# One of four sums of activations: from an adding transfer to an add on VectorE, and a longer landing in the planner's table

## The chip, the core and the metric

The kernel runs on one core of a Trainium2 chip. The metric is the device time of one execution in microseconds; the time before is 1039.71 us, the median of three runs (1039.67 to 1039.81). TensorE's granted clock was 0.999 of its full rate in the profiled execution.

## The reference

Three stages follow one another, all in float32.

1. Attention over channels: q, k and v are 6016 x 256. The columns of q and k are divided by their norm over the 6016 rows, s = k^T q / tau is 256 x 256, a softmax is taken over its last axis, and v is multiplied by the result.
2. First layer: h = x w_in (256 to 2048 channels), g = h * clip(h + 3, 0, 6) / 6, and g w_out back to 256 channels.
3. Second layer: h = max(x w_in2, 0), and (h * h) w_out2.

```
    h = np.maximum(x @ w_in, 0.0)
    return (h * h @ w_out).astype(np.float32)
```

## The kernel before, in words

**The work.** The tokens are cut into six pairs of blocks, five of 2 x 512 and one of 2 x 448 tokens. A pair goes through the 2048 hidden channels in eight groups of 256. One pair and one group is a unit; the second layer has 48 of them. Every float32 operand is split into a high and a low half (float32r), and a product is three matmuls: high x high, low x high, high x low. A split is made of a copy on ScalarE (the high half) and a subtraction on VectorE (the low half).

Both matrix products of a unit, 2 x 2 blocks each, can be formed by seven products in place of eight from sums of blocks (Strassen's scheme, Winograd's form). From the second pair of the second layer on, first7s (L1558) forms the hidden layer of a unit by seven products p1 to p7 in two PSUM banks, X and Y. ScalarE takes snapshots of a bank into SBUF (snap, L1589), VectorE adds totals from a bank (total, L1595), then the rectifier and the square follow (L1602, L1608 on ScalarE, L1615 on VectorE for one block). The four blocks of the hidden layer stand in four tiles R[0] to R[3]; the tiles of even units are called rs in the trace, those of odd units rp.

**Seven products in the second half of a unit.** In 19 of the 40 such units (even groups; S2SET, L1434) the output product is made by seven products too. It needs four sums of the hidden blocks, here called data sums. tail (L1677) forms them in place, one after the other: t1 = R[1] + R[0] in R[1], t3 = R[0] + R[2] in R[0], t2 = R[1] + R[2] in R[1], t4 = R[3] + R[1] in R[3]. Each sum is split for TensorE (split, L1619: high half L1623, low half L1627) into a tile called gs. A sum overwrites its tile only after the tile's own split has read it. The sums are made by move (L1635): a DMA issued from GpSimd's queue (L1637) that adds its source to its destination, 128 x 512 float32, 256 KB. Here the sums of a unit are four such transfers. t1 waits for the split of R[1] and the square of R[0]; t3 waits for t1; t2 waits for the split of t1; t4 waits for t2. In the list of the planner t2 depends on t3 as well, though it reads nothing that t3 writes.

The tail of unit k is entered in the program when unit k+2 is; its products are placed in unit k+3 (items_sums, L1751): t3's at the beginning, those of t2, t1 and t4, in that order, at the end. The weights' sums for them (w2x) are made ahead of the stretch.

**The order of the work.** Plan (L22) lays out the order of every engine by hand. Each operation has an engine, a cost and a latency (how long after its end its users may start). TensorE and the DMA issues of SyncE keep the order in which the program lists them. For VectorE, ScalarE and GpSimd, issue (L66) runs through the program by these costs: the engine that can start first takes, of its ready operations, the one whose due time is earliest. Due times are reckoned back from the products on TensorE that need the result. The order found is then written out; on the chip each engine runs its list strictly in order and waits for whatever its next instruction needs. A move is entered with a cost of MOVE_US = 0.9 us on GpSimd and a latency of MOVE_LAT = 4.2 us (L155), an operation on VectorE over n columns with dve_us(n) = 0.07 + 0.00104 n, one on ScalarE with act_us(n) = 0.1 + 0.00083 n.

While this goes on SyncE issues the loads of weights (w from w1d, 448 KB each), of the next pair's tokens (xr from x2d, 256 KB each) and the stores of results, on the same 16 DMA engines.

Of the kernel before, what the change touches and what calls it, by code (L numbers as in the profile page):

```python
# [15 lines left out]
ALU = mybir.AluOpType  # L16
# [11 lines left out]
class Plan:  # L28
# [13 lines left out]
    def add(self, eng, cost, fn, *deps, lat=LAT):  # L42

        o = Op(eng, cost, lat, fn, list(deps))
        self.ops.append(o)
        return o
# [91 lines left out]
def dve_us(n):  # L138
    return 0.07 + 0.00104 * n
# [12 lines left out]
    return 0.15 + 0.0012 * n  # L152


MOVE_US, MOVE_LAT = 0.9, 4.2  # L155


def pe_us(n, passes):
# [5 lines left out]
def tile_kernel(  # L164
# [71 lines left out]
    V, A, T_ = nc.vector, nc.scalar, nc.tensor  # L236
    plan = Plan()
    add = plan.add
# [699 lines left out]
    for i in range(NCH):  # L938
        loads = chunk_load(i)
        t0, n = chunks[i]  # L940
# [617 lines left out]
    def first7s(pr, g):  # L1558

        l, n = 1, pairs[pr][1]  # L1560
# [4 lines left out]
        R = sets[g // 2 % len(sets)]  # L1565
        names = ("d0", "d1", "d2", "d3") if even else ("p0", "p1", "p2", "p3")
        X, Y = cells["X"], cells["Y"]
        u = {"n": n, "pr": pr, "g": g, "seven": seven, "R": R}

        def product(into, start, wn, xn, *deps):  # L1570
            p = x_op[l, pr, xn]

            def f():
                wh, wl = w_p["w"][:, 0, OPW[wn]], w_p["w"][:, 1, OPW[wn]]
                xh, xl = p["x"][:, 0, :n], p["x"][:, 1, :n]
                ps = into.ap()[:, :n]
                T_.matmul(ps, wh, xh, start=start, stop=False, skip_group_check=True)  # L1577
                T_.matmul(ps, wl, xh, start=False, stop=False, skip_group_check=True)  # L1578
                T_.matmul(ps, wh, xl, start=False, stop=True, skip_group_check=True)  # L1579

            o = add("PE", pe_us(n, 3), f, w_ok, x_done[l, pr, xn], *deps)
            x_held[l, pr, xn].append(o)
            w1_held[l, pr, g].append(o)
            return o

        def snap(k, bank, mm, *deps):
            return add(
                "ACT", act_us(n),
                lambda: A.activation(R[k].ap()[:, :n], bank.ap()[:, :n], AF.Copy), mm, *deps,  # L1589
            )  # L1590

        def total(k, bank, *deps):
            def f():
                r = R[k].ap()[:, :n]
                V.tensor_tensor(r, bank.ap()[:, :n], r, ALU.add)  # L1595

            return add("DVE", dve_us(n), f, *deps)

        def relu(k, src, *deps):
            return add(  # L1600
                "ACT", act_us(n) + 0.08,
                lambda: A.activation(R[k].ap()[:, :n], src.ap()[:, :n], AF.Relu), *deps,  # L1602
            )

        def square(k, *deps):
            def f():
                r = R[k].ap()[:, :n]
                A.activation(r, r, AF.Square)  # L1608

            return add("ACT", act_us(n), f, *deps)  # L1610

        def both(k, *deps):
            def f():
                r = R[k].ap()[:, :n]
                V.scalar_tensor_tensor(r, r, 0.0, r, ALU.max, ALU.mult)  # L1615

            return add("DVE", dve_us(n), f, *deps)

        def split(k, cell, *deps):  # L1619
            c = cells[cell]  # L1620

            def f_hi():
                A.activation(c.ap()[:, 0, :n], R[k].ap()[:, :n], AF.Copy)  # L1623

            def f_lo():
                x = c.ap()
                V.tensor_tensor(x[:, 1, :n], R[k].ap()[:, :n], x[:, 0, :n].bitcast(F32), ALU.subtract)  # L1627

            hi = add("ACT", act_us(n), f_hi, *deps, c.take())
            lo = add("DVE", dve_us(n), f_lo, hi)  # L1630
            R[k].use(hi, lo)
            c.use(hi, lo)
            return c, hi, lo

        def move(k, j, *deps):  # L1635
            def f():
                nc.gpsimd.dma_start(R[k].ap()[:, :n], R[j].ap()[:, :n], accum_op=ALU.add)  # L1637

            o = add("POOL", MOVE_US, f, *deps, lat=MOVE_LAT)
            R[k].use(o)  # L1640
            R[j].use(o)
            return o

        def steps():
            p1 = product(X, True, "a11", "b11", X.take())
            sn1 = snap(0, X, p1, R[0].take())
            yield
            p2 = product(Y, True, "a12", "b21", Y.take())
            h11 = total(0, Y, p2, sn1)
            Y.use(h11)  # L1650
            g0 = square(0, relu(0, R[0], h11))
            if not seven:
                u[0] = split(0, names[0], g0)
            yield
            p6 = product(X, False, "s2", "t2", sn1)
            sn6 = snap(2, X, p6, R[2].take())
            yield
            p7 = product(Y, True, "s3", "t3", Y.take())
            sn7 = snap(3, Y, p7, R[3].take())
            yield  # L1660
            p5 = product(X, False, "s1", "t1", sn6)
            h22 = total(3, X, p5, sn7)
            g3 = both(3, h22)
            u[3] = split(3, names[3], g3)
            yield
            p4 = product(Y, False, "a22", "t4", sn7)
            h21 = total(2, Y, p4, sn6)
            Y.use(h21)
            g2 = square(2, relu(2, R[2], h21))
            u[2] = split(2, names[2], g2)  # L1670
            yield
            p3 = product(X, False, "s4", "b22", h22)
            r = relu(1, X, p3, R[1].take())
            X.use(r)
            g1 = square(1, r)
            u[1] = split(1, names[1], g1)
            def tail():  # L1677
                t1 = move(1, 0, u[1][1:], g0)
                u["t1"] = split(1, "t1", t1)
                t3 = move(0, 2, t1, g2)  # L1680
                u["t3"] = split(0, "t3", t3)
                t2 = move(1, 2, u["t1"][1:], t3)
                u["t2"] = split(1, "t2", t2)
                t4 = move(3, 1, t2, u[3][1:])
                u["t4"] = split(3, "t4", t4)

            if seven:
                u["tail"] = tail
            yield
# [362 lines left out]
```

## Time and profile before

| what | value |
|---|---|
| median of three runs | 1039.71 us (1039.67 to 1039.81) |
| the profiled execution | 1039.63 us, its span 1037.8 us |
| granted clock of TensorE | 0.999 |
| TensorE busy | 1023.2 us, 4565 matmuls |
| VectorE busy | 858.1 us, 1353 instructions |
| ScalarE busy | 795.0 us, 1287 instructions |
| GpSimd busy | 85.9 us, 97 instructions, of them 76 adding transfers |

The span is the time from the first to the last instruction of the core; the execution's own time is a little longer. An engine's busy time says how much it works, not whether it holds up the others. In the timeline, a bracket at the end of a row gives how long the engine was idle before the instruction and what ended that idle time. Rows of GpSimd's transfers show the time in which the engine issues them; their landing is told apart. Rows of matmuls overlap, since they are pipelined: what counts is the distance between their starts.

### The profile page before, as it was taken

How to read it: one execution, taken by the hardware profiler on the slowest of the kernel's cores; microseconds unless marked ns; L12 is line 12 of the kernel's file. 1: busy time of each engine (PE TensorE's matmuls, PEld its weight loads, DVE VectorE, ACT ScalarE, POOL GpSimd, SP SyncE). 2: the span in 40 equal slices, each digit the busy share in tenths (PEclk: the TensorE clock that was granted, in tenths of full speed). 3: DMA queues.
4: the chain of work that ended last, by engine and by line, in shares of the span. 5: the costliest groups of instructions: out<-in, count | busy, mean ns of one | idle time of the engine just before them, and what ended most of it. 6: DMA issues, size and time to landing. Idle time of an engine off the chain costs nothing.

```text
span 1037.8 us, 13028 instructions
## 1 busy us (share of the span) xinstructions
PE 1023.2 (99%) x4565; PEld 853.0 (82%) x4565; DVE 858.1 (83%) x1353; ACT 795.0 (77%) x1287; POOL 85.9 (8%) x97
## 2 busy tenths in 40 slices
PE   9999999999999999999999999999999999999998
PEld 7888888888888888888998888788777778878897
DVE  3999988889989898898878976788778878868866
ACT  5787667678677777677668878888788879778784
POOL 3400000000000000000000000111111111112110
PEclk9999999999999999999999999999999999999999
DMA  9657346344545545635645334765757675765761
GB/s 357 262 174 247 126 152 228 132 159 166 190 150 168 188 146 170 236 107 205 226 167 181 114 107 132 187 176 147 204 130 170 160 190 138 189 172 136 191 169 46
DMA packets 65345, 178.98 MB, mean 172 GB/s; under 512 B 7296, under 2 KB 10880, under 8 KB 64000
## 3 DMA queue, kind: packets, MB, share of 16 engines
q1 hardware_dynamic: 54336, 158.62, 45.4%
q0 software_dynamic: 10944, 19.53, 10.9%
q8 instruction: 36, 0.59, 0.2%
q14 instruction: 29, 0.24, 0.1%
HBM read 126.35 MB, written 32.24 MB: 153 GB/s over the span
## 4 chain that ended last, share of the span: by engine, by line
PE 69%; issue 14%; DMA 13%; POOL 2%; DVE 1%; ACT 0%; SPq 0%; POOLq 0%
DMA rs<-rs 12%; PE acc L1362 10%; PE acc L1367 10%; PE acc L1361 10%; PE A L1268 4%; PE A L1269 4%; PE A L1270 4%; PE s L900 3%; POOL rs L1637 2%; PE B L1270 2%; PE B L1269 2%; PE B L1268 2%; PE xy L1577 2%; PE xy L1578 2%; PE xy L1579 2%
## 5 line engine op out<-in xcount | busy, mean ns | idle before, releaser
L1361 PE MATMUL acc<-g,wo 128*128 128x512 f32 (+1 forms) x448 | 172.9, 386 | 0.0
L1362 PE MATMUL acc<-g,wo 128*128 128x512 f32 (+1 forms) x448 | 172.9, 386 | 0.0
L1154 DVE TENSOR_TENSOR g<-r,g 128x1024 fp32r<-128x1024 f32 (+1 forms) x112 | 135.0, 1205 | 24.0 <-ACT g L1150 23.8
L1150 ACT ACTIVATE g<-r 128x1024 fp32r<-128x1024 f32 (+1 forms) x112 | 117.1, 1046 | 46.1 <-DVE r L1124 45.4
L1637 POOL DMA_DIRECT2D rs<-rs x76 | 65.7, 864 | 907.6 <-DVE gs L1627 775.2
L1367 PE MATMUL acc<-g,wo 128*128 128x512 f32 (+1 forms) x448 | 136.5, 386 | 0.0
L1627 DVE TENSOR_TENSOR gs<-rs,gs 128x512 fp32r<-128x512 f32 (+1 forms) x137 | 90.3, 674 | 42.3 <-ACT gs L1623 40.8
L1623 ACT ACTIVATE gs<-rs 128x512 fp32r<-128x512 f32 (+1 forms) x137 | 80.4, 614 | 22.1 <-DMA rs<-rs 16.0
L1362 PEld LDWEIGHTS acc<-g,wo 128*128 128x128 f32 x448 | 84.1, 188 | 16.1
L1361 PEld LDWEIGHTS acc<-g,wo 128*128 128x128 f32 x448 | 84.1, 188 | 16.1
L1367 PEld LDWEIGHTS acc<-g,wo 128*128 128x128 f32 x448 | 84.1, 188 | 16.1
L1119 ACT ACTIVATE r<-hp,three 128x1024 f32<-128x1024 f32 (+1 forms) x40 | 45.3, 1132 | 49.0 <-DVE hp L1301 48.9
L1577 PE MATMUL xy<-xt,w 128*128 128x512 f32 (+1 forms) x160 | 64.0, 400 | 7.4 <-ACT rs L1589 4.5
L1293 ACT ACTIVATE hp<-A 128x512 f32<-128x512 f32 (+1 forms) x96 | 56.6, 589 | 9.6 <-PE A L1270 8.6
L1578 PE MATMUL xy<-xt,w 128*128 128x512 f32 (+1 forms) x160 | 61.7, 386 | 0.0
L1579 PE MATMUL xy<-xt,w 128*128 128x512 f32 (+1 forms) x160 | 61.6, 385 | 0.0
L1124 DVE SCALAR_TENSOR_TENSOR r<-r,hp 128x1024 f32<-128x1024 f32 (+1 forms) x40 | 47.9, 1197 | 15.8 <-ACT r L1119 15.5
L1627 DVE TENSOR_TENSOR gs<-rp,gs 128x512 fp32r<-128x512 f32 (+1 forms) x80 | 52.5, 671 | 5.8 <-ACT gs L1623 5.1
L1707 PE MATMUL acc<-gs,wo 128*128 128x512 f32 (+1 forms) x141 | 54.3, 385 | 0.0
L1708 PE MATMUL acc<-gs,wo 128*128 128x512 f32 (+1 forms) x141 | 54.3, 385 | 0.0
L1709 PE MATMUL acc<-gs,wo 128*128 128x512 f32 (+1 forms) x141 | 54.2, 385 | 0.0
L1623 ACT ACTIVATE gs<-rp 128x512 fp32r<-128x512 f32 (+1 forms) x80 | 49.1, 615 | 4.5 <-DVE rp L1615 4.0
(375 smaller groups left out, 2595.3 us busy)
## 6 DMA issues: line engine op xcount, KB each, us to landing
w<-w1d SPq DMA_DIRECT2D x176, 448.0 KB, 4.3
rs<-rs POOLq DMA_DIRECT2D x64, 256.0 KB, 3.5
qk<-in_qk_dram SPq DMA_DIRECT2D x8, 1024.0 KB, 16.3
w1d<-wA SPq DMA_DIRECT2D x16, 448.0 KB, 5.3
xr<-in_vT_dram SPq DMA_DIRECT2D x5, 1024.0 KB, 6.8
x2d<-o SPq DMA_DIRECT2D x20, 256.0 KB, 3.9
w1d<-wA SPq DMA_DIRECT2D x16, 256.0 KB, 2.6
w1d<-w SPq DMA_DIRECT2D x14, 256.0 KB, 2.7
```

What stands on the lines that cost most here:

```text
L1150: A.activation(t["g"][:, a:b, 0, :n], t["t"][:, a:b, :n], AF.Copy)
L1154: V.tensor_tensor(g[:, a:b, 1, :n], t["t"][:, a:b, :n], g[:, a:b, 0, :n].bitcast(F32), ALU.subtract)
L1268: T_.matmul(ps, wh, xh, start=start, stop=False, skip_group_check=True)
L1361: T_.matmul(acc[b, e][:, :n], w(e, 0), gh_, start=first_of, stop=False)
L1362: T_.matmul(acc[b, e][:, :n], w(e, 1), gh_, start=False, stop=False)
L1367: T_.matmul(acc[b, e][:, :n], w(e, 0), gl_, start=False, stop=last_of_b)
L1577: T_.matmul(ps, wh, xh, start=start, stop=False, skip_group_check=True)
L1578: T_.matmul(ps, wl, xh, start=False, stop=False, skip_group_check=True)
L1579: T_.matmul(ps, wh, xl, start=False, stop=True, skip_group_check=True)
L1623: A.activation(c.ap()[:, 0, :n], R[k].ap()[:, :n], AF.Copy)
L1627: V.tensor_tensor(x[:, 1, :n], R[k].ap()[:, :n], x[:, 0, :n].bitcast(F32), ALU.subtract)
L1637: nc.gpsimd.dma_start(R[k].ap()[:, :n], R[j].ap()[:, :n], accum_op=ALU.add)
```

## The change

The first of the four data sums, t1, is no longer a transfer but a tensor_tensor of VectorE, in place, with the same two tiles and the same dependencies: it is entered with dve_us(n) as its cost and the ordinary latency. t3, t2 and t4 stay transfers. The readers and writers of both tiles are told of the add as they were told of the transfer. And MOVE_LAT, the landing with which the planner enters each of the remaining transfers, goes from 4.2 to 6.2 us.

```diff
-MOVE_US, MOVE_LAT = 0.9, 4.2
+MOVE_US, MOVE_LAT = 0.9, 6.2
...
             def tail():
-                t1 = move(1, 0, u[1][1:], g0)
+                def f_t1():
+                    r = R[1].ap()[:, :n]
+                    V.tensor_tensor(r, r, R[0].ap()[:, :n], ALU.add)
+
+                t1 = add("DVE", dve_us(n), f_t1, u[1][1:], g0)
+                R[0].use(t1)
+                R[1].use(t1)
                 u["t1"] = split(1, "t1", t1)
                 t3 = move(0, 2, t1, g2)
                 u["t3"] = split(0, "t3", t3)
```

The products on TensorE, their order, and the DMA issues of SyncE are the same as before.

## Rows read from the trace of the kernel before

**Rows 1.** The page: span, and busy time, share and instructions of each engine.

```profile
span 1037.8 us, 13028 instructions
PE 1023.2 (99%) x4565; PEld 853.0 (82%) x4565; DVE 858.1 (83%) x1353; ACT 795.0 (77%) x1287; POOL 85.9 (8%) x97
```

**Rows 2.** Windows: busy us (instructions) of each engine, granted clock, DMA share, GB/s.

```profile
core 0: us, PE busy (x) PEld busy (x) DVE busy (x) ACT busy (x) POOL busy (x), PEclk, DMA share, GB/s
650.00:1000.00 350.00, 342.61 (x1509) 280.55 (x1508) 277.70 (x447) 289.71 (x538) 60.37 (x70) 1.00 0.67 168
```

**Rows 3.** Waits of TensorE: us in total, times, longest us.

```profile
PE xy L1577 <- ACT rs L1589: 4.5, 3, 2.3
PE xy L1577 <- ACT rp L1589: 2.5, 3, 1.3
```

**Rows 4.** Timeline, TensorE: start us, us, instruction [idle before, what ended it].

```profile
750.71 0.39 PE L1708 MATMUL acc<-gs,wo 128*128 128x512 f32 x1
750.94 0.39 PE L1709 MATMUL acc<-gs,wo 128*128 128x512 f32 x1
753.62 0.50 PE L1577 MATMUL xy<-xt,w 128*128 128x512 f32 x1 [2.29 <-ACT rs L1589]
753.96 0.39 PE L1578 MATMUL xy<-xt,w 128*128 128x512 f32 x1
```

**Rows 5.** Timeline, ScalarE, same stretch.

```profile
752.45 0.63 ACT L1623 ACTIVATE gs<-rs 128x512 fp32r<-128x512 f32 x1 [3.32 <-DMA rs<-rs]
752.99 0.58 ACT L1589 ACTIVATE rs<-xy 128x512 f32<-128x512 f32 x1
```

**Rows 6.** Timeline, GpSimd, the unit's first two transfers.

```profile
737.95 0.86 POOL L1637 DMA_DIRECT2D rs<-rs  x1 [4.67 <-DVE gs L1627]
745.28 0.86 POOL L1637 DMA_DIRECT2D rs<-rs  x1 [6.47 <-DMA rs<-rs]
```

**Rows 7.** Transfers: the page's group, landing of all, and that issued at 745.28.

```profile
L1637 POOL DMA_DIRECT2D rs<-rs x76 | 65.7, 864 | 907.6 <-DVE gs L1627 775.2
...
DMA to landing us min/median/max: 3.2/3.5/8.3
...
rs<-rs POOLq DMA_DIRECT2D x1, 256.0 KB, 7.1
```

**Rows 8.** Waits of ScalarE for the transfers, 636 to 1034 us.

```profile
ACT gs L1623 <- DMA rs<-rs: 16.0, 12, 3.3
```

**Rows 9.** Timeline, TensorE: the other four long stalls.

```profile
805.52 0.50 PE L1577 MATMUL xy<-xt,w 128*128 128x512 f32 x1 [1.28 <-ACT rp L1589]
...
845.21 0.50 PE L1577 MATMUL xy<-xt,w 128*128 128x512 f32 x1 [0.87 <-ACT rp L1589]
...
918.43 0.50 PE L1577 MATMUL xy<-xt,w 128*128 128x512 f32 x1 [2.04 <-ACT rs L1589]
...
949.16 0.50 PE L1577 MATMUL xy<-xt,w 128*128 128x512 f32 x1 [0.39 <-ACT rp L1589]
```

**Rows 10.** Timeline, ScalarE: the splits ahead of those four stalls.

```profile
804.35 0.63 ACT L1623 ACTIVATE gs<-rs 128x512 fp32r<-128x512 f32 x1 [1.68 <-DMA rs<-rs]
...
844.04 0.63 ACT L1623 ACTIVATE gs<-rs 128x512 fp32r<-128x512 f32 x1 [2.57 <-DMA rs<-rs]
...
917.26 0.63 ACT L1623 ACTIVATE gs<-rs 128x512 fp32r<-128x512 f32 x1 [3.10 <-DMA rs<-rs]
...
947.99 0.63 ACT L1623 ACTIVATE gs<-rs 128x512 fp32r<-128x512 f32 x1 [0.78 <-DMA rs<-rs]
```

**Rows 11.** Timeline, GpSimd and TensorE: an undisturbed unit's first transfer, its last sum's product.

```profile
698.03 0.86 POOL L1637 DMA_DIRECT2D rs<-rs  x1 [5.32 <-DVE gs L1627]
...
725.11 0.39 PE L1707 MATMUL acc<-gs,wo 128*128 128x512 f32 x1
```

**Rows 12.** Groups by line and shape, VectorE: busy us, mean ns, idle before.

```profile
L1627 DVE TENSOR_TENSOR gs<-rs,gs 128x512 fp32r<-128x512 f32 x112 | 75.5, 686 | 37.5 <-ACT gs L1623 36.2
...
L1627 DVE TENSOR_TENSOR gs<-rs,gs 128x448 fp32r<-128x448 f32 x25 | 14.9, 620 | 4.8 <-ACT gs L1623 4.6
```

**Rows 13.** Waits of the weight loads for VectorE's totals, 636 to 1034 us.

```profile
PEld xy L1577 <- DVE rs L1595: 2.5, 10, 0.3
```

## The prediction, on record before the change was run

> **What bounds the kernel now.** I read the page's head first: TensorE is busy 1023.2 of the span's 1037.8 us [rows 1], so whatever is won must come from the few microseconds in which it is not fed. The profiled execution took 1039.63 us, 1.83 us more than its span, and lies 0.08 us under the median of the runs, 1039.71; the sum below is made against it. The table of windows comes next, over the stretch in which the four data sums are formed (650 to 1000 us): TensorE 342.61 of 350 us, VectorE 277.70 with 447 instructions, ScalarE 289.71, and a granted clock of 1.00 [rows 2]. So 7.4 us of idle TensorE lie in this stretch, no engine beside it is full, and the clock is no part of the story.
>
> The view of waits says what those 7 us are. TensorE waited for ScalarE's snapshots (L1589, the copy of a product out of PSUM) six times in all, 4.5 and 2.5 us [rows 3]. The timeline shows the longest: matmuls start 0.23 us apart, then one starts 2.68 us after its predecessor, marked as 2.29 us of waiting [rows 4]. A matmul's row lasts 0.39 us and overlaps the next by 0.16, so the loss is 2.29 + 0.16 = 2.45 us, and the matmul after it starts 0.34 instead of 0.23 us later, 0.11 more. The price of such a stall is its idle time plus 0.27 us.
>
> Why was the snapshot late? On ScalarE it starts at 752.99, right behind a split (L1623) that began at 752.45 after 3.32 us of idling for a landing of "rs<-rs", an adding transfer [rows 5]. ScalarE runs in order: a split whose transfer is late holds up the snapshot behind it, and the snapshot holds TensorE. On GpSimd's queue that transfer is the second of its unit (t3): it could be issued at 745.28 only, 6.47 us of waiting after the first (t1, at 737.95), because t1 had not landed before [rows 6]. It then took 7.1 us itself, where the median transfer takes 3.5 and the worst 8.3 [rows 7]. The planner had reckoned with 0.9 + 4.2 = 5.1 us from issue to landing. ScalarE's waits for these landings come to 16.0 us in 12 places [rows 8]; most are hidden from TensorE, but the other four long stalls of TensorE, 1.28, 0.87, 2.04 and 0.39 us [rows 9], each have a split right ahead of them on ScalarE that waited for "DMA rs<-rs": 1.68, 2.57, 3.10 and 0.78 us [rows 10].
>
> **The change part by part.**
>
> *Transfer t1 goes.* 19 of the 76 transfers (one per unit formed by seven products) leave GpSimd's queue. What they cost there, 0.864 us each in the page's group [rows 7], lies on an engine that is busy 60 of 350 us and costs nothing. What matters is the start of the others: t3 reads and overwrites what t1 read, and t2 needs the split of t1. Both now start after a VectorE add instead of a landing of 3.2 to 8.3 us. In the worst unit t3 would have been issued near 738.6, not 745.28, and even at 7.1 us would have landed near 746, 6 us before the 752.45 at which ScalarE got it. Next in line there is the snapshot itself, which waits for its own product only. For t4, the transfer of three of the five stalls, the step counts too: it follows t2, which follows the split of t1.
>
> *The longer landing.* Each of the three transfers left is planned at 0.9 + 6.2 = 7.1 us. The planner lays ScalarE's order out by these times, so a split goes behind some four more instructions of ScalarE than before (2 us at about 0.52 us between starts). Only a landing over 7.1 us can then hold the engine, by at most 8.3 - 7.1 = 1.2 us [rows 7] instead of 3.2. Moreover the plan lets t2 wait for t3's landing, which the chip does not: t2 has no data from t3. So t2 and t4 run ahead of their plan by most of a landing, and only t3 stands in plan as early as in fact. Could the longer plan run into the products that use the sums? In an undisturbed unit t1 is issued at 698.03 and the last sum's product starts at 725.11 [rows 11], 27.1 us. The planned chain becomes 0.6 (add) + 3 x 7.1 + 1.4 (last split, both halves) = 23.3, where four transfers made 4 x 5.1 + 1.4 = 21.8. It fits with 3.8 us to spare; in the last pair, with 448 columns for 512, the same stretch is about 23.7 us (an estimate by that ratio), which just fits. Cost 0; if it did not fit, splits would be planned a microsecond late in three units, up to 3 us.
>
> *The added VectorE add.* 19 adds of two SBUF operands and an SBUF result. The nearest rows are VectorE's own low-half subtractions of the same operands, 0.686 us at 512 columns and 0.620 at 448 [rows 12]: 16 x 0.686 + 3 x 0.620 = 12.8 us of VectorE time. Upper bound: all of it in TensorE's way, +12.8 us. Lower bound: all of it in VectorE's 350 - 278 = 72 us of idle time, 0; below nothing it can't be by itself. It waits for no transfer: the low half of u1's split precedes it on VectorE, and the square of R0 was made earlier in the unit. Behind it in the queue stand the totals of L1595, and on two of three in a unit TensorE waits (the first frees bank Y for the seventh product, the one of h22 frees X for the third). How tight they are the weight loads show: 10 waits for them, 2.5 us, none over 0.3 [rows 13]. Two units (20.3 us) have about 447 x 20.3 / 350 = 26 VectorE instructions, 4 of them such totals, so an add put in at random stands right ahead of a tight one in 4 of 26 cases and costs up to its length: 19 x 4/26 x 0.69 = 2.0 us. I take 2.0, nearer to the lower end because the planner hands VectorE first what is due first, and the totals are due before the add.
>
> *A rule that bears on the longer landing.* The rows give 3.2 to 8.3 us for 256 KB [rows 7]. The Trainium skill (DMA: Bandwidth & Descriptors, section "Anatomy of one DMA — SWDGE (gpsimd) path") gives a transfer issued by GpSimd some 2.0 us plus its bytes at 436 GB/s; for 256 KB that would be 2.6 us, an estimate from that page, and by it no landing would ever exceed the old plan. The trace does not agree: its shortest is 3.2 us and its longest over three times the page's figure.
>
> *Sum.* Removed: the five stalls, 2.29 + 1.28 + 0.87 + 2.04 + 0.39 = 6.87 us of idle, plus 5 x 0.27, makes 8.2; the sixth wait of the same kind is what is left of 7.0 (0.13), with its 0.27 some 0.4 us. Together 8.6 us. Added: 2.0 us. 1039.63 - 8.6 + 2.0 = 1033.0 us.
>
> **The rivals.**
> 1. *The waits move.* ScalarE's order is laid out anew, and a split or a snapshot comes to stand behind something else that is late: 57 transfers remain, they still share the DMA engines with the loads of weights and tokens, and a landing of 7 us stays possible. For it: ScalarE waited in 12 places and only five of them struck TensorE, so which ones strike is partly chance. Against: both halves of the change add distance at every one of these places. If stalls worth three of the six come back, 3/6 x 8.6 = 4.3 us, the time is 1037.3, and between 1035.5 and 1040.
> 2. *The add delays the totals* (the other side). If the add stands ahead of the first total of the next unit in most tails, the seventh product starts one add later, 0.6 us (the spacing of VectorE's instructions) in each. 8.6 / 0.6 = 14.3: from 15 of the 19 units on, the change loses; in all 19 it costs 11.4 and gives 1039.63 - 8.6 + 11.4 = 1042.4. For it: u1's split ends just where the next unit's first total comes up. Against: 0.69 us on an engine with a fifth of its time free, and the totals' earlier due.
> 3. *No gain.* The landing is not what holds ScalarE; the wait shown is only the last of several, the change takes nothing away, and the add costs its 2.0: 1041.6. Against it: in the five places the idle time of ScalarE, its split, its snapshot and TensorE's matmul follow one another within 1.2 us. The page's 2.6 us, were it true here, would lead to this case.
>
> **How the numbers follow.** Forecast 0.70 (1029 to 1036, most likely 1033.0); the waits move 0.17; the add delays 0.08; no gain 0.05. A measurement of this kernel tells 0.2%, 2.1 us, from no change, so faster means under 1037.6 and slower over 1041.8. The first case is all faster; of the second a little over half, 0.09; so faster 0.79. The same: the rest of the second (0.08) and parts of the other two (0.05), 0.13. Slower: 0.08. The range starts at 1028.5, where nearly all of the 8.6 us is won, the add costs nothing and the weight loads' small waits shrink with it (another 2.5 us), and ends at 1040.0, the end of the second case; the two last cases are left out.
>
> **What would show it.** Right: GpSimd issues 57 transfers; 19 adds of about 0.69 us stand on VectorE, which is some 13 us busier; TensorE's waits for L1589 fall from 7.0 to under 2 us and ScalarE's for "DMA rs<-rs" from 16 to under 4; t3 is issued within 2 us of the add. TensorE's weight loads wait for L1595 some 2 us more in sum. Wrong: ScalarE's waits for landings stay above 8 us; or they go, and TensorE waits for VectorE's totals in their place; or the span shrinks by less than TensorE's idle time does.

## The result and the profile after

The changed kernel takes 1030.91 us, the median of four runs (1029.68 to 1031.12), against 1039.69 us for the kernel before beside it: a ratio of 0.9916 with a 95% interval of 0.9898 to 0.9933, 8.8 us less. Run again in a later set (e9 below) it had 0.9892 (0.9867 to 0.9917). The forecast was 1033.0 in a range of 1028.5 to 1040.0. One execution of the later runs, the first of e2, took 1720.98 us at a mean granted clock of 0.556; it counts in no ratio here, and its profile is not read.

The profiled execution took 1029.68 us. Its head, as [rows 1], and the stretch of [rows 2]:

```profile
span 1027.9 us, 13018 instructions
PE 1020.8 (99%) x4565; PEld 854.9 (83%) x4565; DVE 866.5 (84%) x1372; ACT 795.3 (77%) x1287; POOL 69.4 (7%) x78
...
650.00:1000.00 350.00, 348.93 (x1551) 289.29 (x1550) 289.84 (x473) 295.56 (x549) 45.23 (x53) 1.00 0.59 158
```

VectorE has 19 instructions more, GpSimd 19 fewer, and TensorE's idle time in the stretch is 350 - 348.93 = 1.07 us where it was 7.39.

The 4565 matmuls come in the same order in both kernels, so the starts can be laid side by side. Of the 9.9 us by which the last one starts earlier, 2.0 are there before 630 us, 1.3 of them in the first 50 us, where both kernels run the same instructions: this is how two executions differ, and luck of this pair (the runs of the kernel before include one of 1038.53 us). The other 7.9 us come after 630 us, most of them at the stalls of [rows 4] and [rows 9]: 2.45 us at the matmul that started at 753.62, 2.22 at that of 918.43, 1.44 at 805.52. In e9's profile of the same kernel the gain after 630 us is 8.1.

All of TensorE's waits after (who waited for what: us in total, times, longest), where [rows 3] had 7.0 us for L1589:

```profile
PE warm L928 <- DVE ebias L841: 1.1, 1, 1.1
PE aTp L1049 <- ACT at L1035: 0.8, 1, 0.8
PE xy L1577 <- DVE rp L1595: 0.7, 1, 0.7
PE acc L1713 <- DVE c L1827: 0.2, 1, 0.2
```

ScalarE's waits from 636 us on are the first three below and four smaller ones; the row of [rows 8], 16.0 us for "DMA rs<-rs", has no successor.

```profile
ACT rp L1589 <- PE xy L1579: 23.5, 27, 1.5
ACT rp L1602 <- DVE rp L1595: 12.1, 13, 2.3
ACT rs L1589 <- PE xy L1579: 9.1, 28, 0.7
```

The unit of [rows 6] on VectorE and GpSimd. L1680 is the new add; 0.54 us after its end the transfer of t3 is issued, at 737.80, where before it waited for t1's landing until 745.28. All 19 adds show this distance, but for the first with 0.60.

```profile
736.58 0.68 DVE L1680 TENSOR_TENSOR rs<-rs 128x512 f32<-128x512 f32 x1
...
737.80 0.86 POOL L1637 DMA_DIRECT2D rs<-rs  x1 [7.96 <-ACT rp L1602]
744.70 0.86 POOL L1637 DMA_DIRECT2D rs<-rs  x1 [6.03 <-DVE gs L1627]
749.34 0.86 POOL L1637 DMA_DIRECT2D rs<-rs  x1 [3.78 <-DMA rs<-rs]
```

The name in the bracket of 737.80 is misleading: the add is what the transfer waits for, as the same distance in all the units shows, and another semaphore that came a little later by the profile got the credit. The adds (duration min/median/max) and the landing of the 57 transfers, as [rows 7] and [rows 12]:

```profile
L1680 DVE TENSOR_TENSOR rs<-rs x19: 615/681/686, 638.7 to 992.0; 128x512 f32<-128x512 f32 x16, 128x448 f32<-128x448 f32 x3
...
DMA to landing us min/median/max: 3.1/3.3/7.1
```

What the change has put in place of the old stalls is seen in VectorE's timeline at 834 us. An add stands right ahead of a total of L1595 that TensorE needs, and a little later a token load (xr) holds L780 and with it the next totals:

```profile
834.64 0.68 DVE L1680 TENSOR_TENSOR rs<-rs 128x512 f32<-128x512 f32 x1
835.24 0.68 DVE L1595 TENSOR_TENSOR rp<-xy,rp 128x512 f32<-128x512 f32 x1
838.44 0.69 DVE L780 TENSOR_TENSOR xt<-xr 128x512 f32<-128x512 f32 x1 [2.52 <-DMA xr<-x2d]
...
839.65 0.68 DVE L1595 TENSOR_TENSOR rp<-xy,rp 128x512 f32<-128x512 f32 x1
```

TensorE beside it: after the add's total the seventh product starts on time at 835.97, and only the matmul behind it is 0.11 us late (0.34 for 0.23); after the token load there is a stall of 0.72 + 0.16 us and the 0.11 behind it.

```profile
835.73 0.39 PE L1715 MATMUL acc<-gs,wo 128*128 128x512 f32 x1
835.97 0.50 PE L1577 MATMUL xy<-xt,w 128*128 128x512 f32 x1
836.31 0.40 PE L1578 MATMUL xy<-xt,w 128*128 128x512 f32 x1
...
840.39 0.50 PE L1577 MATMUL xy<-xb,w 128*128 128x512 f32 x1 [0.72 <-DVE rp L1595]
```

### The profile page after: what moved, and what is told of

Read it like the earlier page. It is cut to its first block, busy times and chain, and to the rows that moved or that the text cites. A ratio compares the mean times of both kernels' runs of the same rounds, so it can differ in the third digit from the quotient of the medians.

```text
span 1027.9 us, 13018 instructions
## 1 busy us (share of the span) xinstructions
PE 1020.8 (99%) x4565; PEld 854.9 (83%) x4565; DVE 866.5 (84%) x1372; ACT 795.3 (77%) x1287; POOL 69.4 (7%) x78
## 4 chain that ended last, share of the span: by engine, by line
PE 95%; DVE 2%; ACT 1%; DMA 1%; issue 0%; SPq 0%; DVEq 0%
PE acc L1361 10%; PE acc L1362 10%; PE acc L1367 10%; PE xy L1577 6%; PE xy L1579 6%; PE xy L1578 6%; PE A L1268 4%; PE A L1269 4%; PE A L1270 4%; PE s L900 4%; PE acc L1713 3%; PE acc L1715 3%; PE acc L1714 3%; PE B L1268 2%; PE B L1270 2%; PE B L1269 2%
## 5 line engine op out<-in xcount | busy, mean ns | idle before, releaser
L1637 POOL DMA_DIRECT2D rs<-rs x57 | 49.2, 862 | 915.8 <-ACT rp L1589 607.5
L1577 PE MATMUL xy<-xt,w 128*128 128x512 f32 (+1 forms) x160 | 63.1, 395 | 0.1
L1595 DVE TENSOR_TENSOR rp<-xy,rp 128x512 f32<-128x512 f32 (+1 forms) x60 | 40.4, 674 | 17.3 <-ACT rp L1589 14.2
```

## The experiments

The change has two halves, and the prediction took both for steps in one direction. So the first set does each half alone, doubles the add, and moves it off VectorE. The table gathers all twelve runs; the ratio is to the kernel before on the same chip in the same set, and the last column is TensorE's idle time from 650 to 1000 us of the profile (350 less the busy time; 7.39 before, 1.07 with the change).

| label | t1 | planned landing | ratio (95% interval) | TensorE idle, us |
|---|---|---|---|---|
| e1_landing_only | transfer | 6.2 | 1.0156 (1.013 to 1.0182) | 13.20 |
| e2_add_only | VectorE | 4.2 | 0.9933 (0.9909 to 0.9958) | |
| e3_add_twice | VectorE, twice | 6.2 | 0.996 (0.9941 to 0.998) | 6.16 |
| e4_add_on_gpsimd | GpSimd | 6.2 | 0.9875 (0.9856 to 0.9893) | 0.31 |
| e5_landing_8p2 | VectorE | 8.2 | 1.0192 (1.016 to 1.0223) | 17.99 |
| e6_landing_t2_free | transfer | 6.2 | 0.9896 (0.9869 to 0.9923) | 1.92 |
| e7_add_only_again | VectorE | 4.2 | 0.9926 (0.99 to 0.9953) | 3.66 |
| e8_all_on_gpsimd | GpSimd, as all sums | none | 0.9968 (0.9956 to 0.998) | 4.30 |
| e9_change_again | VectorE | 6.2 | 0.9892 (0.9867 to 0.9917) | 0.90 |
| e10_gpsimd_again | GpSimd | 6.2 | 0.9873 (0.9847 to 0.9898) | 0.24 |
| e11_gpsimd_t2_free | GpSimd | 6.2 | 0.9882 (0.9856 to 0.9908) | 0.29 |
| e12_gpsimd_tokens_late | GpSimd | 6.2 | 0.9868 (0.9839 to 0.9898) | 0.25 |

The ratios need one caution. The kernel before does not run at the full clock in every execution: in these three sets (e1 to e4, e5 to e8, e9 to e12) its mean granted clock lies between 0.993 and 1.000 and its time between 1037.21 and 1047.55 us, by and large the longer the lower the clock. Its medians are 1041.53, 1043.39 and 1041.42 us; of the executions at 0.999 or more alone they would be 1040.4, 1039.0 (a single one) and 1039.6. So a part of each lead, 1 to 4 us, is clock that the kernel before lost. At 0.999 or more on one chip the change (e9) is at 1030.4 us for 1039.6, a gain of 9.2 us instead of 11.0.

**The longer landing alone**

```diff
-MOVE_US, MOVE_LAT = 0.9, 4.2
+MOVE_US, MOVE_LAT = 0.9, 6.2
```

> Only the longer planned landing (6.2 for 4.2 us); t1 stays a transfer, so 76 transfers. Theory (the late landings cost what they do because the plan has no room for them, and either half of the change makes room): ScalarE's waits for landings fall from 16.0 to under 5 us, TensorE's waits for snapshots from 7.0 to under 3 us, and the time is 1031 to 1035 us. Against it stands that four planned transfers of 7.1 us and the last split make 29.8 us, more than the 27.1 us between the first transfer and the last sum's product: splits then come late in the plan. Rival (it is the shorter chain, the add in place of t1, that makes the room): the time stays over 1037 us.

Measured: 1058.47 us, slower by 1.6%. ScalarE no longer waits for any landing and TensorE no longer waits for a snapshot behind one, as the theory said. But a new wait has come. TensorE's waits, and the timeline of one of them on TensorE and ScalarE:

```profile
PE acc L1707 <- ACT gs L1623: 15.8, 10, 2.9
PE acc L1709 <- DVE gs L1627: 1.6, 4, 0.5
```

```profile
706.70 0.39 PE L1709 MATMUL xy<-gs,w2x 128*128 128x512 f32 x1
708.49 0.50 PE L1707 MATMUL acc<-gs,wo 128*128 128x512 f32 x1 [1.40 <-ACT gs L1623]
...
706.26 0.62 ACT L1602 ACTIVATE rp<-rp 128x512 f32<-128x512 f32 x1
706.78 0.62 ACT L803 ACTIVATE xb<-xr 128x512 fp32r<-128x512 f32 x1
707.30 1.14 ACT L1623 ACTIVATE gs<-rs 128x512 fp32r<-128x512 f32 x2
```

ScalarE is busy with other work right up to the split that TensorE waits for, and its row bears no wait: the data were there. The two transfers issued one behind the other from 699.87 on (the second is this unit's t4) landed 3.8 us after their issue (median), at 703.2 and 704.7 us:

```profile
699.87 1.75 POOL L1637 DMA_DIRECT2D rs<-rs  x2 [9.41 <-DVE gs L1627]
...
rs<-rs POOLq DMA_DIRECT2D x2, 256.0 KB, 3.8
```

So nothing is late on the chip. The plan is: four transfers of 7.1 us and a split make 29.8 us, more than the 27.1 between the first transfer and the last sum's product [rows 11]. The planner lets TensorE wait in its own reckoning, finds the split early enough behind other work, and the chip obeys. The planned times show it (Plan is plain arithmetic on the listing and gives them without a chip): in e1's plan TensorE waits for t4's split in 17 of the 19 units, 29.7 us in all; in the plan of the kernel before and in that of the change it never does, not in the last pair either. The theory's time was wrong, and the rival's "over 1037" was right but far too mild. Not all of the loss is waiting: the clock falls five times behind these stalls, which is worth some 8 us of e1's profile (last section).

**The add alone**

```diff
-MOVE_US, MOVE_LAT = 0.9, 6.2
+MOVE_US, MOVE_LAT = 0.9, 4.2
```

(against the changed kernel).

> Only the add on VectorE; the landing stays planned at 4.2 us, so 57 transfers. Theory (either half makes room): the two stalls behind t3 (2.45 and 2.2 us with the matmul after them) go, those behind t4 shrink; ScalarE's waits for landings fall to 3 to 9 us; time 1032 to 1036 us, a little over the whole change. Rival (the longer planned landing alone does it, the add only costs VectorE): over 1037 us, ScalarE still waits more than 9 us for landings.

> The add alone with 4.2 us once more, for its profile. ScalarE should still wait for landings, in t3's and t4's places, 3 to 9 us in all (16.0 before, none with the whole change), and TensorE for snapshots behind them 1 to 4 us; ratio 0.991 to 0.996. If ScalarE doesn't wait for landings at all, the longer landing did its work by another way than by keeping ScalarE from waiting.

Measured: 0.9933 and 0.9926, as the theory had it. The profile of e7 shows what the longer landing still has to do. ScalarE's and TensorE's rows:

```profile
ACT gs L1623 <- DMA rs<-rs: 7.3, 7, 3.0
...
PE xy L1577 <- ACT rp L1589: 3.5, 4, 1.4
```

7.3 of the 16.0 us of waiting are left, and 3.5 of the 7.0 us of TensorE. The add alone wins more than half, the longer landing the rest; but alone the longer landing loses 1.6%. The two halves don't add up, and the next two runs ask why.

**Does the planned chain fit?** With the add, 0.6 + 3 x 7.1 + 1.4 = 23.3 us fit the 27.1. The test takes the fit away while the add stays, and gives the fit while t1 stays a transfer.

```diff
 e5, against the changed kernel:
-MOVE_US, MOVE_LAT = 0.9, 6.2
+MOVE_US, MOVE_LAT = 0.9, 8.2
 e6, against the kernel before:
-MOVE_US, MOVE_LAT = 0.9, 4.2
+MOVE_US, MOVE_LAT = 0.9, 6.2
-                t2 = move(1, 2, u["t1"][1:], t3)
+                t2 = move(1, 2, u["t1"][1:], g2)
```

> The whole change with 8.2 us as the planned landing in place of 6.2. Theory (a landing must be planned so that the chain of a unit's sums still fits between its first sum and its last sum's product, 27 us): 0.6 + 3 x 9.1 + 1.4 = 29.3 us does not fit, so TensorE waits for the last sum's split (L1623 ahead of the product of t4) as with the longer landing alone, 1 to 2 us in most units, and the kernel is slower than before, ratio 1.003 to 1.016. Rival (with t1 out of the transfers, more room is only safer): ratio under 0.995, as with 6.2.

> Four transfers as before, landing planned at 6.2 us, and t2 entered in the plan without its dependence on t3 (no data ties them). The planned chain is then t1, its split, t2, t4: 3 x 7.1 + 2 x 1.4 = 24.1 us, which fits the 27 us, where the landing alone made 29.8. Theory (it is the fit of the planned chain that turned the longer landing from a loss to a gain, not the add as such): TensorE no longer waits for t4's split, ScalarE's waits for landings stay under 5 us, ratio 0.990 to 0.996. Rival (as long as t1 is a transfer, the longer landing costs): ratio over 1.003.

Measured: 1.0192 for the chain of 29.3 us, 0.9896 for that of 24.1. TensorE's first rows with 8.2 us, then ScalarE's only row for transfers with t2 free:

```profile
PE acc L1713 <- ACT gs L1623: 11.3, 11, 3.1
PE acc L1715 <- DVE gs L1627: 6.5, 10, 1.1
```

```profile
ACT gs L1623 <- DMA rs<-rs: 0.2, 1, 0.2
```

Both ways the theory holds. In the planned times TensorE waits for t4's split in 12 units and 28.6 us with 8.2 us, and in a single unit (1.35 us) with t2 free. A chain that does not fit costs 17 to 19 us whether or not the add is there; one that fits lets the longer landing do its work, and then, with all 76 transfers still in place, the kernel is as fast as the changed one within the intervals. So beside the longer landing the add counts by shortening the planned chain by 7.1 - 0.6 us; taking away the dependence of t2 on t3, which no data needs, did as well. With the old landing (e7) the chain, 0.6 + 3 x 5.1 + 1.4 = 17.3 us, fits with much to spare, and there the add gains by letting the next transfers start early.

**The add doubled**

```diff
                     V.tensor_tensor(r, r, R[0].ap()[:, :n], ALU.add)
+                    V.tensor_tensor(r, r, r, ALU.max)
```

> The whole change, and right behind each of the 19 adds a second VectorE instruction of the same shape (the maximum of R[1] with itself, in place), which the planner does not know of: 12.7 us more of VectorE. Theory (the totals behind the add have about half a microsecond in hand, which one add uses up): each of the 11 units where a total follows the add at once loses most of 0.6 us, the others little: 5 to 8 us more than the whole change, 1036 to 1039 us. Rival (VectorE's idle time hides such instructions wherever they stand): under 1033 us. That difference is what a VectorE instruction costs at this place once the room is gone.

Measured: 1037.44 us, 6.5 over the changed kernel's 1030.91 (another set; by the ratios 0.996 and 0.9916 it is 4.6, which the clock of the kernel before blurs). TensorE waits for L1595 ten times, where eleven were expected:

```profile
PE xy L1577 <- DVE rp L1595: 5.9, 10, 0.8
```

One of the ten, on VectorE and TensorE, where L1681 is the second instruction:

```profile
676.80 0.69 DVE L1680 TENSOR_TENSOR rs<-rs 128x512 f32<-128x512 f32 x1
677.52 0.69 DVE L1681 TENSOR_TENSOR rs<-rs 128x512 f32<-128x512 f32 x1
678.13 0.68 DVE L1595 TENSOR_TENSOR rp<-xy,rp 128x512 f32<-128x512 f32 x1
...
678.87 0.50 PE L1577 MATMUL xy<-xt,w 128*128 128x512 f32 x1 [0.58 <-DVE rp L1595]
```

Here the second instruction costs its whole time, 0.58 + 0.16 us. In the changed kernel the add stands right ahead of such a total in 10 of 19 units and costs 0.1 us in eight of them, 0.3 in one (at 916.94) and next to nothing in one, 1.3 us in all against e10's profile, where the same matmuls are on time: it uses up what the total has in hand, to the last tenth.

**The add on GpSimd**

```diff
-                    V.tensor_tensor(r, r, R[0].ap()[:, :n], ALU.add)
+                    nc.gpsimd.tensor_tensor(r, r, R[0].ap()[:, :n], ALU.add)
...
-                t1 = add("DVE", dve_us(n), f_t1, u[1][1:], g0)
+                t1 = add("POOL", pool_us(n), f_t1, u[1][1:], g0)
```

> The whole change, but the add of t1 is a tensor_tensor of GpSimd (1.3 us at this width in the part of the kernel before that uses it) in place of one of VectorE. Theory (what counts is that t1 is early and certain, and VectorE's share costs 1 to 2 us): VectorE has 19 instructions fewer than with the whole change, the weight loads wait less for L1595, time 1029 to 1031.5 us. Rival (a GpSimd add and VectorE's instructions with two SBUF operands get in each other's way): the adds last over 1.5 us or VectorE's instructions grow from 0.68 us, and the time is over 1032 us.

> The whole change as it is, on the chip of the runs beside it, for comparison. Ratio 0.990 to 0.993 (0.9916 before).

> The add of t1 on GpSimd once more, beside the whole change on one chip. If the place ahead of VectorE's totals costs the whole change its 1.5 to 2 us, this is 1.5 to 4 us under it, ratio 0.986 to 0.990. Rival (the two differ by the chip they ran on): within 1 us of the whole change.

Measured: e4 1028.15 us (0.9875); side by side on one chip 1028.69 (e10) and 1030.44 (e9, the change). The medians differ by 1.75 us, within what was expected; the ratios' intervals overlap. The add lasts 1.67 us here (first row, of e4): over the 1.5 that the rival named, but without the rival's time. The weight loads' waits for L1595, 4.8 us in 15 places with the change (second row, e9), are 1.2 in 5 (third, e10):

```profile
L1680 POOL TENSOR_TENSOR rs<-rs 128x512 f32<-128x512 f32 x16 | 26.7, 1671 | 680.1 <-DVE gs L1627 680.1
```

```profile
PEld xy L1577 <- DVE rp L1595: 4.8, 15, 1.0
```

```profile
PEld xy L1577 <- DVE rp L1595: 1.2, 5, 0.3
```

So VectorE's 12.8 us for the adds cost the change 1 to 2 us.

**All four sums on GpSimd**

```diff
-                nc.gpsimd.dma_start(R[k].ap()[:, :n], R[j].ap()[:, :n], accum_op=ALU.add)
+                r = R[k].ap()[:, :n]
+                nc.gpsimd.tensor_tensor(r, r, R[j].ap()[:, :n], ALU.add)
...
-            o = add("POOL", MOVE_US, f, *deps, lat=MOVE_LAT)
+            o = add("POOL", 0.15 + 0.003 * n, f, *deps)
```

(against the kernel before).

> All four sums as adds of GpSimd (planned at 0.15 + 0.003 n us, 1.69 us, after the 1.67 us measured for t1), no transfer at all. Theory (what costs is the uncertain landing and, with VectorE, its time): no wait of ScalarE for a landing, no add ahead of VectorE's totals, ratio 0.984 to 0.988. Rival (GpSimd's adds and VectorE's two-operand instructions slow each other): the adds last over 2 us or VectorE's subtractions over 0.72 us, ratio over 0.990.

Measured: 0.9968, and the rival's ratio is right: at 1039.61 us nothing is gained over the kernel before at full clock. The adds stay under the 2 us that the rival named (1.15 to 1.79). VectorE's instructions that read two operands from SBUF are stretched when they begin while a GpSimd add runs: 1.55 us for L1615 in the timeline, 0.69 before; the total (L1595), which reads one operand from SBUF and one from PSUM, keeps its 0.69 beside the same adds. The row of GpSimd is two adds one behind the other, 1.29 us each.

```profile
642.44 0.69 DVE L1595 TENSOR_TENSOR rp<-xy,rp 128x512 f32<-128x512 f32 x1 [1.02 <-ACT rp L1589]
643.17 1.55 DVE L1615 SCALAR_TENSOR_TENSOR rp<-rp 128x512 f32<-128x512 f32 x1
...
641.50 2.66 POOL L1638 TENSOR_TENSOR rs<-rs 128x512 f32<-128x512 f32 x2 [601.82 <-DVE gs L1627]
```

From 636 us on 54 of VectorE's instructions are longer than 0.76 us, by 36 us together; with one add a unit on GpSimd (e4) there are five, since of VectorE's instructions that run beside that add most are totals or began before it.

**Two steps further**

```diff
 e11, against e4:
-                t2 = move(1, 2, u["t1"][1:], t3)
+                t2 = move(1, 2, u["t1"][1:], g2)
 e12, against e4:
-                        add("DMA", 0.73, ..., free, x2_stored[pr], tuple(load), lat=MID)
+                        add("DMA", 0.73, ..., free, x2_stored[pr], tuple(load), lat=FAR)
```

> The add of t1 on GpSimd, landing 6.2 us, and t2 entered without its dependence on t3: the planned chain is 1.3 + 1.4 + 2 x 7.1 + 1.4 = 18.3 us of 27. Theory (once the chain fits, more room changes nothing): within 1.5 us of the add on GpSimd alone. Rival (the room left over is still worth something in the last pair, where the stretch is 24 us): 1.5 us or more under it.

> The add of t1 on GpSimd, and the four part loads of the next pair's tokens planned with 6.0 us to landing in place of 3.0. With the whole change the longest stall left, 0.88 us at 840 us, came from a token load that landed late in front of VectorE's L780, which held a total of L1595. Theory (it is the same mechanism with another transfer): VectorE's waits for xr go, and with them about 1 us; ratio 0.001 under the add on GpSimd. Rival (planning these loads longer moves the order elsewhere): no gain, or a loss of 1 us or more.

Measured: 1029.67 and 1028.14 us, beside 1028.69 for the add on GpSimd alone. Freeing t2 changes nothing once the chain fits, as expected. With the token loads planned longer VectorE's wait for xr, 1.8 us in e10, is gone, and the median is 0.55 us lower, which the runs (1027.19 to 1029.29 and 1028.18 to 1029.36) don't tell apart. e12 is the fastest of all: 1028.14 us, against 1030.44 for the change and 1041.42 for the kernel before in the same set; its lead over the change, 2.3 us, is larger than the spread of its own runs, but the two intervals overlap.

## Why the prediction was right, point by point

- **What bounds.** Right, and shown twice: the stalls of TensorE were waits of ScalarE for late landings. With the change ScalarE's 16.0 us and TensorE's 7.0 us are both zero; with the add alone (e7) 7.3 and 3.5 are left. The forecast had asked for under 4 and under 2.
- **t1 goes.** Right: t3 is issued 0.54 us after the add.
- **The longer landing.** The mechanism was right, the fallback was not. The text worked out that the chain of 23.3 us fits the 27.1 and put the price of a chain that doesn't at up to 3 us. e1 and e5 measure it: 17 us (1058.47 - 1041.53) and 19 us (1062.71 - 1043.39), with waits in ten and eleven of the units and not in three (1 to 3 us in most) and with falls of the clock. What the text passed over is that four transfers at 7.1 us would not have fitted, that is, that the halves depend on each other.
- **The add on VectorE.** 2.0 us were taken; moving it to GpSimd gives 1.75 us back, and the matmuls behind the adds are late by 1.3 in all. The size was right by luck, for the way was another: the place was not random, and the totals' earlier due did not keep the add behind them. The planner puts the add right ahead of the first total in 10 of the 19 units, as the second rival feared, and the total turns out to have about 0.6 us in hand. e3 shows the rival's price one instruction further on, some 0.74 us in each of ten units. The weight loads of L1577 wait 5.0 us for L1595 where it was 3.1, near the 2 us more of the forecast; VectorE is busy 8.4 us longer by the page (866.5 for 858.1) and not 13: the lengths of its rows sum to 12.4 us more, but neighbours overlap, and the page counts an overlap once.
- **The sum.** After 630 us the matmuls gain 7.9 us where 8.6 - 2.0 = 6.6 was forecast. The difference of 1.3 us is mostly in the term for what is removed: besides the six marked waits, three short delays behind the same kind of late landing, at 721, 784 and 886 us, below what the view of waits lists, went too, 0.23 + 0.31 + 0.26 us and 0.11 behind each, 1.1 us.
- **The rivals.** "The waits move" was nearly right in one place: the token load at 838 us is the same mechanism with another transfer, on VectorE, and costs 1.0 us in the profile. "No gain" is refuted by e6: with the 76 transfers kept and only their plan changed, ScalarE's wait for landings is all but gone, and TensorE's with it. The estimate of 2.6 us for a landing is refuted by every trace: the shortest landing in any of them took 3.1.

What stays open is why single landings take twice the median. The changed kernel has fewer transfers, and its longest landing is 7.1 us for 8.3; but the number is not the cause. The landings (minimum, median, maximum) of e1 and e6 with all 76 transfers, then of e7 with 57:

```profile
DMA to landing us min/median/max: 3.1/3.3/6.0
```

```profile
DMA to landing us min/median/max: 3.1/3.4/7.6
```

```profile
DMA to landing us min/median/max: 3.1/3.3/8.3
```

Over the 5.1 us of the old plan are 18 of 76 landings before, 3 of 76 in e1, 16 of 76 in e6, 10 of 57 in e7 and 3 of 57 with the change. So they go with the order, and with it the moments of issue, and a part of what the longer landing gains in the changed kernel is that fewer landings are late at all. e6 shows that the room in the plan works by itself: its landings are about as late as before, and ScalarE waits 0.2 us. What in an order makes landings late no run here separates.

## What to carry to other kernels

An order written out ahead of time is only as good as the latencies it was reckoned with, and both errors cost: too short, and an in-order engine stands before data that are late (7 us here); too long, and work is put late though its data are there (17 us here, the clock's part with it). Before a planned latency is raised, add up the chain it stands in and set it against the time between its first input and its last use; a dependence in the plan that no data needs counts in that sum. An instruction moved to an engine with a fifth of its time free costs its own length less what the next needed instruction behind it has in hand, so look at that one, not at the share.

## What the runs showed of the hardware

**GpSimd and VectorE hold each other up.** In e8 a VectorE instruction with two SBUF operands that begins during a GpSimd add lasts until 0.55 us after the add's end, 1.55 us for 0.69; none of the 46 with a PSUM operand that run beside an add is touched (0.69 us at most). The one that began first is not stretched: in e4 every add begins 0.17 us behind the start of a VectorE subtraction of two SBUF operands, which keeps its 0.68 us, and the add lasts 1.67 us for the 1.28 of e8's shortest adds of this width. The Trainium skill (SBUF — State Buffer, section "Who interferes with whom") says that a VectorE instruction with two SBUF inputs contends with a GpSimd instruction that reads SBUF, and that one with at most one SBUF input does not, outside VectorE's two-port modes. The traces agree on both.

**TensorE's clock after a stall.** In e1, behind the stall that ended at 665.38, matmuls start 0.43 us apart instead of 0.23 for 3 us, and the granted clock of the windows from 667 to 670 and 670 to 680 us is 0.50 (1.2 GHz) and 0.99 (the last row is a window in a later fall):

```profile
662.93 0.39 PE L1709 MATMUL xy<-gs,w2x 128*128 128x512 f32 x1
665.38 0.50 PE L1707 MATMUL acc<-gs,wo 128*128 128x512 f32 x1 [2.05 <-ACT gs L1623]
...
667.34 0.63 PE L1707 MATMUL B<-gs,wo 128*128 128x512 f32 x1
667.76 0.63 PE L1708 MATMUL B<-gs,wo 128*128 128x512 f32 x1
...
667.00:670.00 3.00, 3.00 (x9) 2.32 (x8) 0.00 (x0) 0.60 (x1) 0.86 (x1) 0.50 0.35 63
670.00:680.00 10.00, 10.00 (x45) 8.23 (x44) 5.48 (x9) 7.48 (x14) 0.00 (x0) 0.99 0.48 139
...
793.20:796.50 3.30, 3.30 (x10) 2.53 (x9) 1.31 (x3) 1.44 (x3) 0.62 (x2) 0.50 0.51 100
```

The eight or nine slow matmuls cost another 1.7 us. The same happens four times more, at 793, 878, 964 and 1005 us, each time within 2 us behind a stall, so the clock takes some 8 us of e1's profile (an estimate, five times 1.7). The profiled execution of the kernel before shows no such fall behind its own stall of 2.68 us between starts [rows 4], and e5's none behind waits of 1.01 and 0.84 us that follow one another three times, where e1's fall at 793 came behind 1.05 and 0.50; so a stall does not always bring it. Whether the other executions of the kernel before lost their clock (0.993 to 0.998, under the table) behind its stalls no kept trace shows.
